# State added by one whole product, bonus vector spread behind the first token sums, and a new order of loads and steps

One core of one Trainium2 chip. The metric is the device time of one execution in microseconds (us); lower is better. A run counts as slow when it is more than 1.5% above the fastest run of the same kernel; fast runs are compared with fast runs.

## The reference

The kernel computes a linear attention with a decaying state (four batches, 8 heads of 48, 768 tokens) and feeds its output into a token-mixing layer.

```python
# attention, per batch and head; w is the decay, u the bonus vector
for t in range(S):
    cur = einsum('bhd,bhe->bhde', u * k[t], v[t])
    y[t] = einsum('bhd,bhde->bhe', r[t], state + cur)
    state = w[t][..., None] * state + einsum('bhd,bhe->bhde', k[t], v[t])
# token mixing, x = y as (B, S, 384)
wq, wk = x @ w_q, x @ w_k
W_tok  = scale * einsum('bsd,btd->bst', wq, wk)
out    = maximum(einsum('bst,btd->bsd', W_tok, x), 0) @ w_out
```

## The kernel before

It works on 12 blocks of 256 tokens, three to a batch. For each block: `load` fetches w, k, r and v, in this order, 384 KB each, from the sync engine's queue; `log` takes the logarithm of w on ScalarE; `sums` adds the logarithms up over the tokens on TensorE (tiles `cw`); `expk` and `expr` take exponentials of the sums; `kdec` (GpSimd, tile `KdS`) and `rdec` (VectorE, tile `RdS`) decay keys and receptances; `trR` transposes them (`psT`); then come two masked products (`A`, `AmB`), the state (`Sn`, `SB`) and the output `Y`. The bonus takes a second path: `uk1` and `uk2` on GpSimd, `red` on VectorE, `vd` on GpSimd.

```python
ld = ctx.enter_context(tc.tile_pool(name="ld", bufs=3))

def load(n, nm, ap):
    b, m = divmod(n, NU)
    src = ap[b, :, ds(m * C2, C2)]
    t = ld.tile([C, H, D2], F32, name=nm + "G", tag=nm + "G")
    nc.sync.dma_start(out=t, in_=src.rearrange("h (p j) d -> p h (j d)", j=2))
    T[nm, n] = t

def log(n):
    T["lw", n] = LW[n % NB]
    nc.scalar.activation(pad(T["lw", n]), jhd(T["w", n]), ACT.Ln, bias=0.0, scale=LN_SCALE)

def stadd(n, q):                       # adds the old state to the new one, in PSUM
    ...
        SB = T["SB", b, 2 * m + q]
        for hh in range(2):            # two products of 64 columns, side by side
            mm(T["Sn", n][ds(hh * 64, 64), q, 0:DM].rearrange(
                "p (q h d) -> p q h d", h=2, d=D)[:, :, hh],
               ID128[:, ds(hh * 64, 64)],
               SB.rearrange("p (q h d) -> p q h d", h=2, d=D)[:, :, hh], start=False)

def ucast():                           # spreads the bonus vector over 128 partitions
    ups = mtile([C, DM], F32, "ups")
    mm(ups, one, u1)
    nc.vector.tensor_copy(ubc, ups)
```

The order of instructions on each engine comes from a plan: every step has a key, and the steps are issued in the order of their keys. A key is not a time on the chip. It only decides who stands ahead of whom on an engine or in a queue.

```python
start  = [0.42, 8.84, 16.14, ...]                # key of each block; steps add to it
lstart = [-100, -99, -98, -11.4, -9.09, 4.54, 0.63, 6.68, 49.1, 51.23, 17.9, 58.9]
for n in range(NT):
    for i, (nm, ap) in enumerate((("w", w), ("k", k), ("r", r), ("v", v))):
        at(lstart[n] + 0.01 * i, lambda n=n, nm=nm, ap=ap: load(n, nm, ap))
    ...
at(-99.985, uload); at(-99.0, ucast); at(-67.84, wload); at(19.23, wcast)
for _, _, fn in sorted(plan, key=lambda x: x[:2]):
    fn()
```

So the blocks are loaded in the order 0, 1, 2, 3, 4, 6, 5, 7, 10, 8, 9, 11.

## Time and profile before

| | before |
|---|---|
| median of the first three runs | 123.15 us (122.78 to 123.25) |
| span of the profiled run | 122.0 us |
| TensorE busy | 100.1 us, 82% |
| VectorE, GpSimd, ScalarE busy | 91.8, 84.7, 77.2 us |
| TensorE almost without a gap (0.9 us of 56) | from about 44 to 100 us |

To read it: shares over the whole span hide stages. TensorE is the bound in the middle. The front, up to some 42 us, is bound by waits, by GpSimd and by the loads. The prediction shows the lines.

### The profile page before, as it was taken

The page shows a single profiled execution, that of the slowest core. Times are in us where ns is not written, and L with a number is a line of the kernel's source. Part 1 is how long each engine was busy: PE and PEld are TensorE (multiplying, and loading weights), DVE is VectorE, ACT ScalarE, POOL GpSimd, SP SyncE. Part 2 cuts the span into 40 slices and gives each one's busy share as a digit, 9 for nine tenths or more (in the row PEclk, how much of TensorE's full clock was granted, in tenths as well). Part 3 has the DMA queues.
Part 4 walks back from the last instruction along what each step waited for, and adds up shares of the span by engine and source line. Part 5 has one row for each costly group of instructions (what it writes and reads, how often), then busy time and mean ns, then how long its engine had stood idle before and what let it go on. Part 6 is the DMA issues. An engine that isn't in the chain of part 4 may idle for free.

```text
span 122.0 us, 4284 instructions
## 1 busy us (share of the span) xinstructions
PE 100.1 (82%) x1822; PEld 64.6 (53%) x1822; DVE 91.8 (75%) x150; ACT 77.2 (63%) x146; POOL 84.7 (69%) x81
## 2 busy tenths in 40 slices
PE   0193938979898999999999899999999999966800
PEld 0133536557575766757657466576576666532400
DVE  6213596699798978999989998989989777253800
ACT  4236391689779868986685948976478966426000
POOL 8949899995999999599597995967839804000000
PEclk9999996799999999999999999999999999999985
DMA  3999999999999999899839999500552200573092
GB/s 77 322 325 325 323 320 341 292 232 318 236 256 273 288 300 263 230 266 247 245 75 329 348 269 252 149 0 0 134 129 52 82 5 0 129 181 85 24 283 83
DMA packets 54598, 24.66 MB, mean 202 GB/s; under 512 B 51121, under 2 KB 54578, under 8 KB 54578
## 3 DMA queue, kind: packets, MB, share of 16 engines
q1 hardware_dynamic: 52274, 21.24, 64.6%
q10 hardware_dynamic: 2304, 3.15, 9.1%
q8 instruction: 14, 0.23, 0.7%
q14 instruction: 6, 0.05, 0.1%
HBM read 19.66 MB, written 4.72 MB: 200 GB/s over the span
## 4 chain that ended last, share of the span: by engine, by line
PE 68%; ACT 12%; DVE 6%; DMA 3%; POOL 3%; issue 2%; ACTq 1%; SPq 1%; DVEq 0%
PE cw L66 12%; PE Y L66 11%; PE psT L66 10%; PE fps L66 10%; PE Sn L66 5%; PE A L66 5%; PE xt_ps L66 5%; PE qk L66 5%; PE Tps L66 4%; ACT X L130 3%; DMA u<-in_u_dram 3%; DVE AmB L244 3%; ACT XT L130 2%; PE mps L66 2%; POOL uk L250 1%
## 5 line engine op out<-in xcount | busy, mean ns | idle before, releaser
L244 DVE TENSOR_TENSOR AmB<-A,MASK 128x1024 bf16<-128x1024 f32 x24 | 28.8, 1219 | 1.3 <-PE A L66 1.2
L271 POOL TENSOR_TENSOR Vd<-V,diag 128x768 bf16<-128x768 bf16 x12 | 17.7, 1478 | 13.7 <-ACT X L130 3.4
L250 POOL TENSOR_TENSOR uk<-kG,ubc 128x768 f32<-128x768 f32 x12 | 21.8, 1816 | 1.7 <-DVE ubc L486 1.7
L178 ACT ACTIVATE em<-cw,bias 128x384 bf16<-128x384 f32 x24 | 13.0, 580 | 15.6 <-PE cw L66 15.6
L257 POOL TENSOR_TENSOR uk<-uk,rG 128x768 f32<-128x768 f32 x12 | 21.8, 1816 | 0.1
L207 POOL TENSOR_TENSOR KdS<-kG,em 128x768 bf16<-128x768 f32 x12 | 19.7, 1640 | 1.2 <-ACT em L178 1.2
L227 DVE COPY RKT<-psT 128x2048 bf16<-128x2048 bf16 x12 | 14.6, 1217 | 4.0 <-PE psT L66 4.0
L66 PEld LDWEIGHTS <-KdS 64*128 64x128 bf16 (+1 forms) x256 | 10.8, 99 | 9.1 <-POOL KdS L207 3.6
L200 DVE TENSOR_TENSOR RdS<-rG,cw 128x384 bf16<-128x384 f32 x24 | 12.2, 551 | 4.5 <-ACT cw L185 4.5
L66 PE MATMUL fps<-wout_sb,mixT 128*128 128x384 bf16 x72 | 14.6, 328 | 0.1
L302 DVE TENSOR_TENSOR SB<-Sn,pt 128x384 bf16<-128x384 f32 x20 | 11.0, 551 | 4.0 <-PE Sn L66 2.6
L66 PEld LDWEIGHTS <-RKT 48*64 48x64 bf16 (+1 forms) x464 | 10.3, 107 | 7.1 <-issue 4.5
L185 ACT ACTIVATE cw<-cw,bias 128x384 f32<-128x384 f32 x24 | 12.3, 553 | 0.2
L264 DVE TENSOR_REDUCE diag<-uk 128x16 f32<-128x768 f32 x12 | 11.3, 945 | 0.4 <-POOL uk L257 0.4
L155 ACT ACTIVATE logw<-wG 128x768 bf16<-128x768 f32 x12 | 10.2, 851 | 2.1 <-DMA wG<-in_w_dram 2.1
L66 PE MATMUL cw<-logw,BI 128*128 128x384 bf16 x36 | 11.5, 377 | 0.0
L66 PE MATMUL psT<-ID,KdS 128*128 128x128 bf16 x96 | 7.8, 227 | 4.0 <-DVE AmB L244 2.0
L66 PE MATMUL cw<-logw,BS 128*128 128x384 bf16 x36 | 11.0, 363 | 0.0
L66 PE MATMUL A<-RKT 48*64 48x128 bf16 x384 | 10.1, 226 | 0.8 <-ACT X L130 0.8
L130 ACT CAST X<-Y 128x768 bf16<-128x768 f32 x11 | 8.8, 800 | 2.9 <-PE Y L66 2.7
L211 ACT CAST V<-vG 128x768 bf16<-128x768 f32 x12 | 10.0, 841 | 0.0
L130 ACT COPY osb<-fps 128x384 f32<-128x384 f32 x13 | 6.1, 484 | 5.3 <-PE fps L66 2.1
(74 smaller groups left out, 165.1 us busy)
## 6 DMA issues: line engine op xcount, KB each, us to landing
wG<-in_w_dram SPq DMA_DIRECT2D x12, 384.0 KB, 5.5
kG<-in_k_dram SPq DMA_DIRECT2D x12, 384.0 KB, 5.1
rG<-in_r_dram SPq DMA_DIRECT2D x12, 384.0 KB, 4.8
vG<-in_v_dram SPq DMA_DIRECT2D x12, 384.0 KB, 4.9
out_dram<-osb ACTq DMA_DIRECT2D x16, 192.0 KB, 3.0
out_dram<-osb SPq DMA_DIRECT2D x8, 192.0 KB, 3.8
wout_f<-in_moe_w_out_dram SPq DMA_DIRECT2D x1, 576.0 KB, 4.7
wq_f<-in_moe_w_q_dram SPq DMA_DIRECT2D x1, 96.0 KB, 4.1
```

The lines of the kernel that those rows point to most:

```text
L66: nc.tensor.matmul(o, l, rr, start=start, stop=stop, skip_group_check=True, is_transpose=trans)
L130: (nc.scalar.copy if e else nc.vector.tensor_copy)(o, i)
L178: nc.scalar.activation(em[:, j], T["cw", n, 1 + j][:, 0:DM], ACT.Exp, bias=bias[2 + j], scale=-1.0)
L185: nc.scalar.activation(cw, cw, ACT.Exp, bias=bias[j], scale=1.0)
L200: nc.vector.tensor_tensor(pad(Rd)[:, j], jhd(T["r", n])[:, j], T["cw", n, j][:, 0:DM].rearrange("p (h d) -> p h d", d=D), ALU.mult)
L207: nc.gpsimd.tensor_tensor(pad(T["Kd", n]), jhd(T["k", n]), hd(T["em", n]), ALU.mult)
L227: nc.vector.tensor_copy(RKT, T["psT", n])
L244: nc.vector.tensor_tensor(T["AmB", n][:, js].rearrange("p q h t -> p h q t"), T["A", n, js], _rep(_rep(MASK[:, js], 1, NP), 1, 2), ALU.mult)
L250: nc.gpsimd.tensor_tensor(uk, T["k", n].rearrange("p h (j d) -> p h j d", j=2), _rep(ubc.rearrange("p (h d) -> p h d", d=D), 2, 2), ALU.mult)
L257: nc.gpsimd.tensor_tensor(uk, uk, T["r", n].rearrange("p h (j d) -> p h j d", j=2), ALU.mult)
L264: nc.vector.tensor_reduce(diag.rearrange("p j h -> p h j"), T["uk", n], axis=AX.X, op=ALU.add)
L271: nc.gpsimd.tensor_tensor(Vd, T["V2", n], _rep(T["diag", n], 3, D), ALU.mult)
```

## The change

The intent has three parts. The addition of the old state becomes one full product instead of two half ones. The product that spreads the bonus vector moves behind the first token sums, and the first decayed keys (`kdec`) go ahead of the first bonus product (`uk1`), so that the first transposes could start earlier. Finally the whole plan is reordered, with the loads and the division of copies between ScalarE and VectorE.

```diff
-            for hh in range(2):
-                mm(T["Sn", n][ds(hh * 64, 64), q, 0:DM].rearrange(
-                    "p (q h d) -> p q h d", h=2, d=D)[:, :, hh],
-                   ID128[:, ds(hh * 64, 64)],
-                   SB.rearrange("p (q h d) -> p q h d", h=2, d=D)[:, :, hh], start=False)
+            mm(T["Sn", n][:, q, 0:DM], ID128, SB, start=False)
...
-    EX = (1, 1, 1, 1, 1, 1, 1, 1, 1, 1, 1, 0)      # 1: ScalarE copies X of this block
-    ET = (1, 1, 1, 1, 0, 0, 0, 0, 0, 1, 1, 0)      # the same for XT
+    EX = (0, 1, 1, 1, 1, 1, 1, 1, 1, 1, 1, 0)
+    ET = (0, 1, 1, 0, 0, 0, 0, 0, 1, 0, 1, 0)
...      (other such lists, every key of the steps, two checks of order, the layout of XT: left out)
     first = [                                      # keys of block 0
...
-        (0.59, uk1, ()),
-        (1.7, expr, ()),
-        (3.15, kdec, ()),
+        (-0.86, expr, ()),
+        (3.93, kdec, ()),
+        (5.41, rdec, ()),
+        (6.11, uk1, ()),
...
-    lstart = [-100, -99, -98, -11.4, -9.09, 4.54, 0.63, 6.68, 49.1, 51.23, 17.9, 58.9]
+    lstart = [-100, -99, -98, -37.57, -37.75, -19.78, -26.05, -25.0, 20.07, 36.92, -5.83, 30.2]
...
-    at(-99.0, ucast)
-    at(-67.84, wload)
-    at(19.23, wcast)
+    at(-5.72, ucast)
+    at(-74.79, wload)
+    at(15.4, wcast)
```

The new `lstart` loads the blocks in the order 0, 1, 2, 4, 3, 6, 7, 5, 10, 8, 11, 9.

## The prediction

> **What bounds the kernel now.** I read the page first: engine totals, then the slices, then the chain that ended last in order of time, then a table of windows, then the timeline of single engines. A block below is 256 tokens of one batch; there are 12, numbered 0 to 11, each passing through loads, exponentials, transposes, two masked products, the state and the output.
>
> ```profile
> PE 100.1 (82%) x1822; PEld 64.6 (53%) x1822; DVE 91.8 (75%) x150; ACT 77.2 (63%) x146; POOL 84.7 (69%) x81
> ```
>
> No engine is full over the span, so the averages hide stages. The windows (stretch, length, then busy us with counts of PE, PEld, DVE, ACT, POOL, then clock, DMA share, GB/s) separate them:
>
> ```profile
> 6.00:12.00 6.00, 4.13 (x24) 1.69 (x23) 1.58 (x3) 3.02 (x6) 4.30 (x4) 1.00 1.17 325
> 12.00:18.00 6.00, 4.15 (x58) 2.78 (x57) 4.22 (x5) 3.79 (x8) 5.39 (x4) 1.00 1.17 322
> 18.00:24.00 6.00, 5.30 (x87) 3.71 (x88) 4.03 (x6) 2.72 (x6) 6.00 (x5) 0.72 1.11 323
> ...
> 44.00:52.00 8.00, 8.00 (x161) 5.16 (x159) 6.97 (x11) 7.44 (x16) 6.52 (x5) 1.00 0.97 256
> ...
> 60.00:68.00 8.00, 8.00 (x184) 5.23 (x182) 7.57 (x11) 5.88 (x12) 7.20 (x5) 1.00 0.82 233
> ```
>
> From 44 us TensorE has no gap (8.00 of 8), with VectorE close behind (7.57 of 8 at 60 to 68). Before 24 us TensorE waits, GpSimd fills up (6.00 of 6) and the transfers run at 322 to 325 GB/s. So there are three stages: a front of some 42 us limited by waits, GpSimd and loads; a middle of some 64 us limited by TensorE; a tail. The front in the chain:
>
> ```profile
> 1.85 3.55 DMA u<-in_u_dram
> 5.40 0.14 issue
> 5.53 1.63 PE ups L66 x2
> 7.16 0.02 issue
> 7.18 0.57 DVE ubc L486
> 7.75 0.07 issue
> 7.83 1.81 POOL uk L250
> 9.64 1.60 POOL KdS L207
> 11.24 0.04 issue
> 11.29 1.89 PE psT L66 x16
> ...
> 26.67 0.26 ACT wq_sb L495
> 26.94 0.24 ACT wk_sb L496
> 27.18 1.05 ACT wout_sb L497
> ```
>
> The path starts with the bonus vector: its load, the product that spreads it, its copy, the keys times the bonus, and only then the decayed keys that the first transposes need. The casts of the weights are also on it, 1.55 us.
>
> **What the Trainium skill says.** (1) "TensorEngine Tiling (Array Packing)", Key Properties: changing the tiling mode drains TensorE. The trace agrees. Around one state addition of before (timeline of PE):
>
> ```profile
> 65.83 0.22 PE L66 MATMUL psT<-ID,RdS 128*128 128x128 bf16 x1
> 65.98 0.27 PE L66 MATMUL Sn<-SB,ID 128*64 128x192 bf16 x2
> 66.18 0.34 PE L66 MATMUL cw<-logw,BI 128*128 128x384 bf16 x1
> 66.36 0.33 PE L66 MATMUL cw<-logw,BS 128*128 128x384 bf16 x1
> ```
>
> The last transpose starts 0.15 us before the pair, where transposes of one mode follow each other after 0.056 us (eight of them last 0.61, one 0.22; 0.39/7). (2) "TensorE: Matmul & The Clock Gate", Part 3: outputs in different column groups run at the same time. Agrees: two products of 0.27 us together occupy 0.27 us, and the next starts 0.20 us after the first. (3) Same page, Back-to-back issue gap: N/2.4 + 2.5 ns when warm, 162 ns for N = 384. Agrees: cw products start 0.16 to 0.17 us apart. (4) "DMA: Bandwidth & Descriptors", anatomy of one DMA: about 2 us of each transfer are fixed. The rows here can't split it, but no load of keys landed under 4.0 us after issue (4.0/5.1/6.4, least, median, most).
>
> **The change part by part.**
>
> *State addition.* 16 additions (32 products in the row Sn<-SB,ID) become 16 products of 128 x 384. Streaming gets longer: 384 columns instead of two times 192 side by side, 0.16 against 0.08 us. Switches of mode get fewer. Between transposes and token sums: before 0.15 in, 0.20 out = 0.35; after 0.056 + 0.163 = 0.22, saving 0.136. After the state product (64-row mode) and before a full-array product: before 0.13 + 0.20 = 0.34, after 0.13 + 0.16 = 0.30, saving 0.04. Between two products of 64-row mode a switch is added: 0.13 + 0.16 + 0.095 = 0.39, losing 0.055 (0.095 is 0.15 less 0.055). In the new order of instructions I count 6 of the first kind, 4 of the second, 3 of the third, and three mixed ones worth -0.04, -0.04 and +0.06. Sum: -0.82 - 0.16 + 0.165 - 0.02 = -0.84 us; counting only blocks 4 to 11, where TensorE is the bound, about -0.45. The other reordering leaves the number of switches as it was (159 with the old addition, 141 with the new).
>
> *Front.* The first logarithm ends at 4.98, so the sums can start about 5.05 instead of 7.08, 2.0 us earlier. In before the second em (the exponential for the keys) ended 2.3 us after the sums' start (7.08 to 9.38); so em is done at 7.4, and the first decayed keys at 7.4 + 1.64 = 9.04 instead of 11.23. That is the intended gain, 2.2 us. But the bonus product now follows the sums (2.35 us, to 7.4) and takes its 1.63, then the copy 0.57: ubc is there at 9.6, where GpSimd, free at 9.04, waits 0.6. Its sequence then, with 1.81 for each product with the bonus or r, 1.64 for KdS, 1.48 for Vd: uk done 11.5, 13.3, 15.1, 16.9, keys of block 1 at 18.5, Vd 20.0, two uk of block 2 23.6, keys of block 2 25.2, Vd 26.7, two uk of block 3 30.3, Vd 31.8, keys of block 3 33.4, and keys of block 4 40.1. In before the keys were ready at 17.0, 25.0, 33.1 and 39.7. GpSimd as a whole is thus not ahead: the keys now come after both bonus products, and eat the lead. The transposes of blocks 3 and 4 began at 34.98 and 41.71, some 1.6 us after my new times, so at most 1.6 us can come out of the front.
>
> *Loads.* There are three buffers per input. The new order is 0, 1, 2, 4, 3, 6, 7, 5, 10, 8, 11, 9, so block 3 has one transfer group of 4 x 1.2 us ahead of it while the queue is full, and block 5 can be loaded only when block 4's keys are released. With 4.0 us to land: keys of 5 at 44.1, two products and the decay 5.25 us later 49.35; the transposes of block 5 began at 49.37. So by block 5 the lead from the front is about nil. If the keys of block 3 land at 28.4 (the fifth group's key issue 23.46 plus 4.9), GpSimd loses 1.7 more, and block 5 is late by as much. Block 9 has the same handicap (after 8), but GpSimd catches up about 1 us per block by then.
>
> *Moves between engines.* Three evacuations go from ScalarE to VectorE net (one X at 0.96 us instead of 0.80, two XT at 0.55 instead of 0.80), the relu, osb and qk counts stay. VectorE +2.1 us over the span, of which 1.5 falls on block 0, about 24 to 28 us, where it was full; between 60 and 84 us some 1.2 us are taken off it. The weights' casts move into ScalarE's wait before 21.8 us (-1.55 on the old path, though they now wait for the weights, which land about 20.2). Seven fewer stores are issued by ScalarE (about 0.6 each); only those at 105.6 to 106.9 stood on the chain, and X of the last block at 107.46 hid them anyway. The layout of XT moves the same elements in the same products: nothing.
>
> *Tail.* From the last Y (106.5) to 122 the order is nearly unchanged; one of six osb copies goes to ScalarE. I take -0.1.
>
> Sum by the walk: front 0 (-1.6 to +1.7), addition -0.45, tail -0.1: about 122.6. The walk charges every stall and gives nothing for the warm clock, and a new order this broad was most likely kept because it ran at least as well; I move 0.7 us for that, a judgement and not a reading: **121.9 us**.
>
> **Rivals.** (a) *The front gain carries through*: 2.2 + 1.55 us come off the chain and GpSimd's waits vanish. For: TensorE is solid behind it, so each microsecond survives. Against: GpSimd's sequence and DMA at 325 GB/s. It would give 119.5 to 120.5. (b) *Loads become the wait*: block 3 and block 5 late by 1 to 2 us, not regained because TensorE is the bound. For: GpSimd's arithmetic above. Against: 18 to 26 us has some idle transfer time. It would give 123.3 to 124.2. (c) *VectorE becomes the bound* around block 1 through the moved X and XT: for, it is full from 24 to 28 us; against, two state evacuations (0.55 each) now run earlier, in its idle time. +0.5 to 1.0, so 122.5 to 123.
>
> **Range and chances.** The walk's middle is 122.6, rival (a) pulls down 2 to 3, (b) up 1. Eight in ten: 120.0 to 123.5. Faster by over 2% needs under 120.7, so rival (a) nearly whole: 0.19. Slower by over 2% needs over 125.6, more than all stalls together: 0.03. Within 2%: 0.78.
>
> **What would show it.** Right if: the first sums start near 5.1, KdS of block 0 ends near 9.1; GpSimd waits about 0.6 for ubc; Sn<-SB,ID is 16 products of 128x384; PE is full from 44 to 100; transposes of block 5 start near 49 with POOL KdS as releaser of a wait of PE or its weight load. Wrong if those transposes start before 47.5 (the front gain held, so 120 us or less), if psT waits elsewhere for loads of block 9, or if TensorE's middle shrinks by over 1 us, which would mean that drains cost more than I counted.

## The result, and the profile after

The changed kernel is slower: 128.17 us, median of 4 runs (126.57 to 128.84), against 122.97 us for the kernel before on the same chip (122.71 to 123.25, 4 runs). The ratio is 1.034, 95% interval 1.0246 to 1.0435. Here and below a ratio is the mean time of one kernel's fast runs over that of the other's fast runs of the same rounds, so it is not quite the ratio of the medians quoted. Two of the four runs (128.84 and 128.58) count as slow; the fast ones took 126.57 and 127.75. The profiled run is the one of 128.84 us, span 126.7 us. What is read from it below was therefore looked for again in fast traces, and it is there (experiments `e2` and `e4`).

The engine totals hardly show where five microseconds went:

```profile
PE 101.7 (80%) x1806; PEld 65.2 (52%) x1806; DVE 94.2 (74%) x153; ACT 75.5 (60%) x143; POOL 85.0 (67%) x81
```

TensorE has 1.6 us more busy time with 16 instructions fewer, VectorE 2.4 us more. The windows after, with the columns the prediction explains, find the place:

```profile
6.00:12.00 6.00, 5.04 (x30) 2.20 (x29) 1.58 (x3) 3.97 (x8) 4.02 (x4) 1.00 1.17 325
44.00:52.00 8.00, 5.80 (x101) 3.22 (x102) 3.46 (x5) 5.63 (x10) 5.51 (x4) 0.79 0.72 193
60.00:68.00 8.00, 8.00 (x147) 5.31 (x146) 8.00 (x13) 4.96 (x10) 7.28 (x5) 1.00 0.73 199
```

The front is busier than before (5.04 instead of 4.13 us of TensorE's time). At 60 to 68 us TensorE is full, as before. But from 44 to 52 us it worked 5.80 us instead of 8.00, with 101 records instead of 161, and the granted clock was 0.79. The waits of the changed kernel (engine, line, what was waited for; total us, times, longest) name the wait:

```profile
ACT logw L157 <- DMA wG<-in_w_dram: 11.7, 6, 4.1
POOL uk L254 <- DMA kG<-in_k_dram: 9.1, 3, 4.5
...
PE cw L68 <- ACT logw L157: 8.9, 3, 5.1
```

ScalarE waited 11.7 us for loads of w; in the kernel before the same group has 2.1 us of idle time. Not all of this is loss: 3.1 us stand ahead of blocks 0 to 2 (a fast run with the old loads, `e6`, has the same 3.1), the rest is 2.96 ahead of block 3, 4.06 ahead of block 5 and 1.62 ahead of block 9. Behind ScalarE, TensorE's token sums waited for the logarithm; of these 8.9 us, 5.1 are the start of block 0, 0.96 block 1 and 2.88 block 5. Up to block 4 the changed kernel is all but level: its transposes of block 4 start at 41.98 us, before at 41.71. The chain that ended last (start, duration, what) puts it in one place, block 5:

```profile
39.36 5.82 DMA wG<-in_w_dram
45.18 0.02 issue
45.20 0.85 ACT logw L157
46.05 0.04 issue
46.09 2.04 PE cw L68 x15
48.13 1.90 PE Y L68 x40
```

One load of w, issued at 39.36 and landed at 45.18, holds up the logarithm, that the sums, and those TensorE. In the kernel before, the same logarithm ran on time; its timeline of ScalarE has it without a wait:

```profile
40.77 0.85 ACT L155 ACTIVATE logw<-wG 128x768 bf16<-128x768 f32 x1
```

The same stretch of the chain of before has no load and no wait in it:

```profile
43.08 1.20 PE cw L66 x15
44.28 1.22 PE Y L66 x40
```

The first sums of block 5 start at 46.09 instead of 42.91 us, which is 3.2 us later. The products behind them are slow on top. From the start of the sums to the start of `Y` it is 1.98 us instead of 1.30, and from there to the next product 1.87 instead of 1.21. (The chain of before enters the sums only at 43.08, because their first 0.17 us lie beside the last transposes; its 1.20 us are therefore not the whole of them.) Together that is 3.2 + 0.7 + 0.7, about 4.5 us, and the transposes of block 5 start 4.7 us later, first after, then before:

```profile
54.02 0.62 PE L68 MATMUL psT<-ID,KdS 128*128 128x128 bf16 x8
```

```profile
49.30 0.62 PE L66 MATMUL psT<-ID,KdS 128*128 128x128 bf16 x8
```

Why the slow products? The timeline of TensorE shows the idle time ahead of the sums, and windows of one microsecond show the clock after it (the third number from the end):

```profile
46.09 0.32 PE L68 MATMUL cw<-logw,BI 128*128 128x384 bf16 x1 [2.88 <-ACT logw L157]
```

```profile
43.00:44.00 1.00, 0.21 (x4) 0.09 (x2) 1.00 (x3) 0.00 (x0) 0.00 (x0) 1.00 1.12 298
...
46.00:47.00 1.00, 0.91 (x4) 0.48 (x4) 0.00 (x0) 1.00 (x4) 0.59 (x1) 0.70 0.54 148
47.00:48.00 1.00, 1.00 (x12) 0.39 (x10) 0.00 (x0) 1.00 (x3) 1.00 (x1) 0.50 0.03 8
49.00:50.00 1.00, 1.00 (x12) 0.30 (x14) 0.83 (x2) 0.25 (x1) 1.00 (x1) 0.59 1.17 325
50.00:51.00 1.00, 0.90 (x24) 0.43 (x23) 0.59 (x1) 0.94 (x3) 1.00 (x2) 1.00 1.14 318
```

The clock reads 1.00, then 0.70, 0.50 and 0.59, and 1.00 again. After 2.88 us without a product and the first sums, TensorE worked at half clock from 46.4 to 49.8 us (worked out from the windows: a mean of 0.70 is 0.60 us at half clock, a mean of 0.59 is 0.82 us). The Trainium skill, "TensorE: Matmul & The Clock Gate", Part 1, says that the array falls to half clock after about one idle window of 3.4 us and warms up after as long a busy one. The trace agrees in the half clock and in its length, 3.4 us (the fast traces of `e2` and `e4` also have 3.4); the idle time ahead of it was shorter than the page says. How much the late start costs and how much the clock is read from the trace; no run separates the two.

Why did w of block 5 come so late? The timeline of the sync engine's queue has its issue, behind block 7's four loads; the second view is the issue of the same w before:

```profile
33.19 1.17 SPq L152 DMA_DIRECT2D wG<-in_w_dram  x1
...
38.23 1.08 SPq L152 DMA_DIRECT2D vG<-in_v_dram  x1
39.36 1.46 SPq L152 DMA_DIRECT2D wG<-in_w_dram  x1
```

```profile
33.60 1.37 SPq L150 DMA_DIRECT2D wG<-in_w_dram  x1
```

The seventh group of loads starts at 33.19 and the eighth at 39.36; before, they start at 33.60 and 39.34. The queue runs at the same pace in both kernels. Only, before, block 5 is the seventh group, and now it is the eighth, since 7 was put ahead of it. That moves its w by 39.36 - 33.60 = 5.8 us, and there were not 5.8 us to spare.

### The profile page after: what moved, and what is told of

Its sections match the earlier page's. It is cut to its first block, busy times and chain, and to the rows that moved or that the text cites. A ratio compares the mean times of both kernels' runs of the same rounds, so it can differ in the third digit from the quotient of the medians.

```text
span 126.7 us, 4242 instructions
## 1 busy us (share of the span) xinstructions
PE 101.7 (80%) x1806; PEld 65.2 (52%) x1806; DVE 94.2 (74%) x153; ACT 75.5 (60%) x143; POOL 85.0 (67%) x81
## 3 DMA queue, kind: packets, MB, share of 16 engines
q10 hardware_dynamic: 1296, 1.77, 5.2%
## 4 chain that ended last, share of the span: by engine, by line
PE 54%; DMA 12%; SPq 9%; ACT 9%; DVE 6%; issue 3%; POOL 1%; DVEq 0%; ACTq 0%; POOLq 0%
PE Y L68 10%; PE cw L68 9%; DMA wG<-in_w_dram 8%; SPq L152 8%; PE fps L68 8%; PE psT L68 8%; PE Sn L68 4%; PE qk L68 4%; DMA rG<-in_r_dram 4%; PE A L68 3%; PE xt_ps L68 3%; ACT X L132 3%; PE Tps L68 2%; PE mps L68 2%; DVE AmB L247 2%
## 5 line engine op out<-in xcount | busy, mean ns | idle before, releaser
L68 PE MATMUL cw<-logw,BI 128*128 128x384 bf16 x36 | 11.7, 384 | 8.9 <-ACT logw L157 8.9
L157 ACT ACTIVATE logw<-wG 128x768 bf16<-128x768 f32 x12 | 10.2, 846 | 12.2 <-DMA wG<-in_w_dram 11.7
L68 PEld LDWEIGHTS <-KdS 64*128 64x128 bf16 (+1 forms) x256 | 11.3, 101 | 6.7 <-issue 2.5
L68 PE MATMUL cw<-logw,BS 128*128 128x384 bf16 x36 | 11.5, 377 | 0.0
L268 DVE TENSOR_REDUCE diag<-uk 128x16 f32<-128x768 f32 x12 | 11.3, 945 | 0.0
L132 ACT CAST X<-Y 128x768 bf16<-128x768 f32 x10 | 8.0, 798 | 3.3 <-PE Y L68 3.3
L418 ACT ACTIVATE mixT<-mps 128x384 bf16<-128x384 f32 x18 | 8.1, 495 | 2.5 <-PE mps L68 2.4
```

What stands on the lines that cost most here:

```text
L68: nc.tensor.matmul(o, l, rr, start=start, stop=stop, skip_group_check=True, is_transpose=trans)
L132: (nc.scalar.copy if e else nc.vector.tensor_copy)(o, i)
L268: nc.vector.tensor_reduce(diag.rearrange("p j h -> p h j"), T["uk", n], axis=AX.X, op=ALU.add)
```

## The experiments

Each "before" median is on the same chip. Calls ran on different chips: `e1` to `e4`, `e5` to `e8`, `e9` to `e12` and `e13` to `e16` belong together.

The theory after reading the trace: the order of loads alone makes the loss. The rivals: the moved bonus product and key order, the copies moved to VectorE, or too few load buffers.

**e1: the changed kernel with the loads in the old order.**

```diff
-    lstart = [-100, -99, -98, -37.57, -37.75, -19.78, -26.05, -25.0, 20.07, 36.92, -5.83, 30.2]
+    lstart = [-100, -99, -98, -11.4, -9.09, 4.54, 0.63, 6.68, 49.1, 51.23, 17.9, 58.9]
```

> The changed kernel with only the list of load times put back to that of before (blocks loaded 0,1,2,3,4,6,5,7,10,8,9,11). Theory L (the new load order is the whole loss: w of block 5 lands at 45.2 us and w of block 9 at 76.3 us, and each wait lets TensorE go idle and cold): 121.0 to 123.0 us, no DMA wait of a logarithm after the first, TensorE without a gap from 44 us. Theory S (the new order on the engines, keys after both bonus products, X and XT of block 0 on VectorE, loses the time, and the loads are only where it shows): still 126 or more. A share for both: 123.5 to 125.5.

Measured: fast runs 123.78 and 123.68 us, before 123.54; ratio 1.0015 (0.9958 to 1.0071). Two more runs were slow (126.84 and 134.24). The loss is gone, so it sits in `lstart`. What remains of the change is worth nothing within 0.6%. Two fast runs are few, but `e6` and `e7` below, which have the same old loads, bear it out with six fast runs each.

The run of 134.24 us is the profiled one. Its window from 60 to 68 us has a granted clock of 0.75 where other runs have 1.00, and this went on to the end.

```profile
60.00:68.00 8.00, 8.00 (x127) 5.03 (x125) 7.22 (x11) 3.92 (x8) 5.61 (x4) 0.75 0.67 179
```

**e2: the kernel before with the loads in the new order** (the same line, the other way round).

> The kernel before with only the list of load times of the change. Theory L: 126 to 129 us, with the logarithm of block 5 waiting 3 to 5 us for its w. Theory S: within 1% of before, 122 to 124.2, since the keys come early in this order and give their buffer back early. A share for both: 124.3 to 126.

Measured: 128.41, 129.28 and 128.70 us fast, 130.96 slow; median 128.99, before 123.54; ratio 1.0425 (1.0373 to 1.0477). One line of keys makes the kernel before as slow as the changed one, and a little slower. Its trace is of a fast run and its chain shows the same wait:

```profile
39.66 5.55 DMA wG<-in_w_dram
...
45.24 0.85 ACT logw L155
```

Here TensorE had been idle for 3.47 us, and all of its sums ran at half clock: they took 2.31 us, and the first ones started 0.27 and 0.32 us apart, where before it was 0.16. With `e1` and `e2` the cause is shown from both sides.

**e3: the kernel before with the whole addition alone.**

```diff
-            for hh in range(2):
-                mm(T["Sn", n][ds(hh * 64, 64), ...  # two products
+            mm(T["Sn", n][:, q, 0:DM], ID128, SB, start=False)
```

> The kernel before with only the state addition as one product of 128x384. The tiling drains saved less the longer streaming: my count gives 0.5 to 0.9 us less, so 122.0 to 122.6 where before has 123.0. If the drains cost nothing and only streaming counts: 0.08 us times 16 more, 124.2. If nothing of it lies on the path: 123.0.

Measured: median of 6 is 122.32 us (121.80 to 122.92), before 123.54; ratio 0.9907 (0.9869 to 0.9945), about 1.15 us. The addition is a real gain of its own. TensorE's timeline shows the working of one addition:

```profile
65.14 0.61 PE L66 MATMUL psT<-ID,RdS 128*128 128x128 bf16 x8
65.58 0.33 PE L66 MATMUL Sn<-SB,ID 128*128 128x384 bf16 x1
65.75 0.33 PE L66 MATMUL cw<-logw,BI 128*128 128x384 bf16 x1
```

The product stands 0.17 us ahead of the token sums; the pair of before stood 0.20 ahead, for half the columns. Read off single starts: from the last transpose to the addition 56 ns instead of 149, and from the addition to the sums 162 instead of 203. The way in is what became cheap.

**e4: the changed kernel with four load buffers.**

```diff
-    ld = ctx.enter_context(tc.tile_pool(name="ld", bufs=3))
+    ld = ctx.enter_context(tc.tile_pool(name="ld", bufs=4))
```

> The changed kernel, its new load order kept, with four buffers per input instead of three. Theory L in its exact form (not the order as such, but that block 5 and block 9 must wait for the buffer of block 4 and block 8): the waits vanish, 121.0 to 123.0 us. If the order itself hurts through the queue (block 4 ahead of block 3 while the transfers are full): about 1.8 us of wait for the keys of block 3 stays and it gives 123 to 124.5. Theory S: 126 or more.

Measured: 127.95, 129.17 and 127.75 us fast, 130.04 slow; median 128.56, before 123.54; ratio 1.0398 (1.0324 to 1.0471). More room does not help. The queue's timeline in this fast run shows why:

```profile
38.40 1.04 SPq L152 DMA_DIRECT2D vG<-in_v_dram  x1
39.49 1.14 SPq L152 DMA_DIRECT2D wG<-in_w_dram  x1
```

w of block 5 is issued at 39.49 as soon as v of block 7 is out, and landed 5.72 us later. It waited for its turn, not for a buffer. The keys of block 5 do need a buffer: with three, they were issued at 41.91 us, right after block 4's keys were released at 41.88. With four they went out at 40.72 and came into use no sooner (46.43 us, with three 46.41). A later wait did vanish: the logarithm of block 9, last in the order, no longer waits (1.62 us with three buffers), and `Y` of block 11 starts at 109.1 instead of 109.9 us, this one against a slow trace; the total shows no gain from it. So the queue bounds block 5 and the buffers block 9.

**e5: the changed kernel, block 5 put ahead of block 7 in the loads.**

```diff
-    lstart = [-100, -99, -98, -37.57, -37.75, -19.78, -26.05, -25.0, 20.07, 36.92, -5.83, 30.2]
+    lstart = [-100, -99, -98, -37.57, -37.75, -25.5, -26.05, -25.0, 20.07, 36.92, -5.83, 30.2]
```

> The changed kernel with one block moved in its load order: 5 ahead of 7, so 0,1,2,4,3,6,5,7,10,8,11,9. Four buffers did not help block 5, whose w still landed at 45.2 us while transfers ran without a pause, so for block 5 it is the place in a full queue and not the buffer. Theory Q (place in the queue): w of block 5 is issued near 33 instead of 39.4, lands before 40 us, TensorE does not stop before the token sums of block 5, and 3 to 4.5 us come back: 123.5 to 125.5 in fast runs; what stays of the wait is block 9 (about 1 us). Theory B (buffer release): nothing changes, 126.5 to 128.8.

Measured: two fast runs, 123.89 and 124.59 us, two slow (127.85 and 126.90); before 123.56. Two fast runs out of four are too few for a ratio with an interval; their mean over the median of before is 1.0055. One number out of the whole plan takes back most of the loss. In the trace (fast) w of block 5 is issued at 33.34, its logarithm runs without a wait, and the sums start at 43.2 us:

```profile
41.18 0.85 ACT L157 ACTIVATE logw<-wG 128x768 bf16<-128x768 f32 x1
```

**e6: e1, with the weights' casts where they were.**

```diff
-    at(15.4, wcast)
+    at(19.23, wcast)
```

> The changed kernel with the old load order, and the casts of the weights put back behind the transposes' copy of block 0 as in before. The first run with the old load order came out level with before although the one-product addition alone brought 0.9%; about 1% is lost elsewhere. If it is the early casts (ScalarE stands 1.9 + 1.8 us for the weights' load and the exponentials of block 2 wait behind it): 0.5 to 1.2 us below the run with old loads alone, so 122.3 to 123.0. If X and XT of block 0 on VectorE are the loss: no change, 123.5, or up to 1 us slower since the casts are then again ahead of the logarithm of block 3.

Measured: 6 fast runs, median 123.78 us, before 123.56; ratio 1.0007 (0.9980 to 1.0033). The early casts, which the prediction credited with 1.55 us "on the old path", bring nothing that can be seen beside `e1`, whose interval is 0.6% to either side.

**e7: e1, with X and XT of block 0 copied by ScalarE again.**

```diff
-    EX = (0, 1, 1, 1, 1, 1, 1, 1, 1, 1, 1, 0)
-    ET = (0, 1, 1, 0, 0, 0, 0, 0, 1, 0, 1, 0)
+    EX = (1, 1, 1, 1, 1, 1, 1, 1, 1, 1, 1, 0)
+    ET = (1, 1, 1, 0, 0, 0, 0, 0, 1, 0, 1, 0)
```

> The changed kernel with the old load order, and X and XT of block 0 evacuated by ScalarE again. In the changed kernel VectorE is full from 24 to 30 us and X and XT of block 0 (0.87 and 0.46 us) stand on the chain between the masks of block 1. If they are the loss: 1.0 to 1.4 us less, 122.1 to 122.6. If the early casts are: no change, 123.5.

Measured: 6 fast runs, median 122.95 us, before 123.56; ratio 0.9950 (0.9918 to 0.9982). That is 0.6% below `e1` (1.0015) and `e6` (1.0007; it differs in the place of the casts too, which brings nothing visible in `e6`), so about 0.75 us; the intervals of `e6` and `e7` just touch. The chain of the changed kernel shows what the two copies cost on VectorE:

```profile
24.47 0.87 DVE X L132
25.34 1.13 DVE AmB L247
26.47 0.46 DVE XT L132
26.94 1.14 DVE AmB L247
```

All four stand on the path one behind the other. With the copies away, in the trace of `e7`, the masks start at 25.25 and 26.66 us, where `e6` has 25.48 and 27.08; they now wait 0.60 and 0.18 us for `A`, so not all of the copies' 1.3 us comes back.

**e8: e3 with the new start: bonus product behind the first sums, first keys ahead of the bonus.**

```diff
-        (0.59, uk1, ()),
         (1.7, expr, ()),
         (3.15, kdec, ()),
+        (3.2, uk1, ()),
...
-    at(-99.0, ucast)
+    at(-5.5, ucast)
```

> The kernel before with the one-product addition and only the new start: bonus product behind the first token sums, first keys decayed ahead of the first bonus product; nothing else moved. If the start is what bounds (chain read as it stands): 2 us less than the addition alone (122.3), so 120.2 to 121. If GpSimd's sequence bounds the front (walk of the prediction: it starts 0.4 us earlier but then waits 0.6 for the bonus): within 0.5 us of 122.3.

Measured: 6 fast runs, median 122.58 us, before 123.56; ratio 0.9919 (0.9889 to 0.9948), the same as `e3`. The first transposes start at 9.0 instead of 11.3 us, and yet nothing is gained: `Y` of block 0 still starts at 23.0 (before 22.9). VectorE's timeline shows where the 2.3 us end:

```profile
14.90 0.95 DVE L264 TENSOR_REDUCE diag<-uk 128x16 f32<-128x768 f32 x1 [2.15 <-POOL uk L257]
15.77 1.01 DVE L200 TENSOR_TENSOR RdS<-rG,cw 128x384 bf16<-128x384 f32 x2
16.70 2.35 DVE L244 TENSOR_TENSOR AmB<-A,MASK 128x1024 bf16<-128x1024 f32 x2
```

The bonus sum of block 0 (`diag`) stands ahead of the masks in VectorE's order. It waits 2.15 us for GpSimd's bonus products, which now come later, and all that stands behind it waits too.

**e9: e8, with the bonus sum of block 0 behind its masks, and `vd` earlier.**

```diff
-        (9.1, red, ()),
         (12.22, mask, (1, )),
+        (12.25, red, ()),
...
+        (14.3, vd, ()),
-        (16.87, vd, ()),
```

> The kernel before with the one-product addition, the new start, and the sum over the bonus product of block 0 moved on VectorE from ahead of the masks of block 0 to behind them (its product with the values moved along on GpSimd). In the run with the new start alone the first transposes begin at 9.0 instead of 11.3 but the masks still at 16.7, because that sum stands ahead of them on VectorE and waits for GpSimd until 14.9. Theory F (VectorE's fixed order hands the lead back): masks of block 0 start near 15.0, transposes of block 1 near 16.5 instead of 18.0, Y of block 0 near 22 instead of 23, and 0.8 to 1.8 us come off: 120.8 to 121.8. Rival (loads or the cold clock of TensorE bound the front): token sums of block 2 stay at 20.7 and the time at 122.4.

Measured: 5 fast runs, 121.85, 121.47, 121.11, 120.69 and 121.60 us, one slow (125.12, the profiled one); before 123.62; ratio 0.9812 (0.9776 to 0.9848). Now the earlier start counts. The order can be seen in the fast trace of `e10`, which has the same one:

```profile
14.10 1.03 DVE L200 TENSOR_TENSOR RdS<-rG,cw 128x384 bf16<-128x384 f32 x2 [1.22 <-ACT cw L185]
15.05 2.35 DVE L244 TENSOR_TENSOR AmB<-A,MASK 128x1024 bf16<-128x1024 f32 x2
17.31 0.94 DVE L264 TENSOR_REDUCE diag<-uk 128x16 f32<-128x768 f32 x1
```

The masks begin at 15.05 instead of 16.70, and `Y` of block 0 starts at 21.5 us in this trace and at 21.0 in that of `e9`, where `e8` had 23.0.

The slow trace of `e9` shows the wait of the changed kernel again, here with the old order of loads. w of block 5 was issued at 36.30 us (before: 33.60), the logarithm waited for it, and TensorE stood idle and then ran at half clock from 44.1 to 47.5 us:

```profile
43.13 0.84 ACT L155 ACTIVATE logw<-wG 128x768 bf16<-128x768 f32 x1 [4.22 <-DMA wG<-in_w_dram]
```

```profile
44.02 0.47 PE L66 MATMUL cw<-logw,BI 128*128 128x384 bf16 x1 [3.04 <-ACT logw L155]
```

**e10: e9, with the cast of the output weights in three parts, placed later.**

```diff
-        nc.scalar.copy(wout_sb, wout_f)
+
+    def wocast(i):
+        nc.scalar.copy(wout_sb[:, i], wout_f[:, i])
...
+    for i, t in enumerate((26.5, 30.3, 33.65)):
+        at(t, lambda i=i: wocast(i))
```

> As the run before it in this list, with the cast of the output weights (1.15 us on ScalarE at 27 us, on the chain ahead of the logarithm of block 3) cut in three and put into ScalarE's gaps behind the logarithms of blocks 3 and 4. If that cast bounds: 0.5 to 1.1 us less again. If the masks on VectorE or the keys on GpSimd bound there: no change.

Measured: median of 6 is 121.87 us (120.93 to 122.29), before 123.62; ratio 0.9844 (0.9803 to 0.9885). No gain over `e9`.

**e11: e9 without the new start**, that is e3 with the moves of `red` and `vd` alone (the same diff as e9, on e3).

> The kernel before with the one-product addition and the moved sum on VectorE, but with the old start (bonus product first). With theory F the lead does not exist here: the masks wait for A at 15.3 to 16.2 and start near 16.0 behind RdS of block 1, as now, at most 0.6 us better: 121.8 to 122.5. If the moved sum alone is worth as much as with the new start (under 121.5), the start has no share.

Measured: 122.04 to 123.77 us, median 122.22, before 123.62; ratio 0.9904 (0.9860 to 0.9948), the same as `e3`. So the start alone gives nothing (`e8`), the order on VectorE alone gives nothing, and the two together give 0.9% more than the addition by itself (`e9` against `e11`, whose intervals just miss each other). The later kernels with both, `e10`, `e13` and `e14`, lie 0.3 to 0.7% below `e11`, so the size of this gain is not settled.

**e12: the changed kernel, with 5 ahead of 7 and 9 ahead of 11 in the loads.**

```diff
-    lstart = [-100, -99, -98, -37.57, -37.75, -19.78, -26.05, -25.0, 20.07, 36.92, -5.83, 30.2]
+    lstart = [-100, -99, -98, -37.57, -37.75, -25.5, -26.05, -25.0, 20.07, 29.0, -5.83, 30.2]
```

> The changed kernel, its own load order but with 5 ahead of 7 and 9 ahead of 11 (0,1,2,4,3,6,5,7,10,8,9,11). If these two places are the whole of the loads' loss: level with the changed kernel on the old load order, 123.3 to 123.9, and no more runs above 126. If block 4 ahead of block 3 also costs (GpSimd waits 1.8 us for the keys of block 3): 0.3 to 1 us above that.

Measured: only two fast runs, 124.62 and 124.31 us, and four slow ones (127.06 to 128.66); median 127.21, before 123.62. The fast mean over the median of before is 1.0068. What still differs in the loads from `e1` is 4 ahead of 3. Its trace (fast) has ScalarE waiting 3.65 us for w of block 3 and GpSimd 2.50 us for its keys. The swap of 9 and 11 shows no gain over `e5` in these few runs.

**e15 and e16: e12 again, one run each, to catch a slow run in a trace.**

> The changed kernel with 5 ahead of 7 and 9 ahead of 11, again, for its trace. If it comes out near 127: the trace shows a wait for block 3's or block 5's data of 3 us or more and TensorE cold behind it (loads), or else PE busy with a lower granted clock throughout (chip). If near 124.5: nothing new.

> As the second look: near 127 with a load's wait of over 3 us if loads make the slower runs, or a low clock throughout if the chip does; near 124.5 tells nothing.

Measured: 124.39 and 124.98 us, correct, the state of single runs unknown; the median of before in this call was 123.41. Neither is as slow as the slow runs of `e12`, so no trace of one exists. Why the kernels with block 4 loaded ahead of block 3 fell into slow runs so often (`e5` 2 of 4, `e12` 4 of 6) stays open. The two kept traces of slow runs with the old order of loads differ: that of `e9` has the late w of block 5, that of `e1` a lower clock and no such wait. So neither the loads nor the clock is shown to be the cause of all of them.

**e13 and e14: the two best kernels with the blocks loaded in their order 0 to 11** (`e13` is `e9`, `e14` is `e10` with this line).

```diff
-    lstart = [-100, -99, -98, -11.4, -9.09, 4.54, 0.63, 6.68, 49.1, 51.23, 17.9, 58.9]
+    lstart = [-100, -99, -98, -11.4, -9.09, 0.63, 4.54, 6.68, 17.9, 49.1, 51.23, 58.9]
```

> The kernel of the start with VectorE's order put right, now with all blocks loaded in their order of use. If the place in the queue is what its slower run (125.1) met: no wait of a logarithm for w after block 2 above 1 us, all runs within 1%, 120.5 to 121.3. If the 125.1 was a slow state of the chip: median as before, 121.5, and again a run near 125.

> The kernel with the split cast of the output weights, with blocks loaded in their order of use. If the loads hid the gain of the split cast (its logarithm of block 5 waited for w until 41.5): 0.5 to 1 us below the run before it in this list, 119.7 to 120.7. If the cast was never on the path: level with it.

Measured against 123.41 us: `e13` median of 6 is 121.91, ratio 0.9878 (0.9843 to 0.9913); `e14` median of 5 is 121.30, ratio 0.9837 (0.9811 to 0.9862). Neither had a slow run, and in the trace of `e13` the logarithm of block 5 does not wait (in `e10`, with the old order, it waits 1.75 us). `e14` is level with `e10`, `e13` lies 0.7% above `e9`, with intervals that just touch: plain order shows no gain, and a small cost is not ruled out. `e9` and `e14` have overlapping intervals, and both beat both kernels: about 1.6 to 1.9% below before. No version is clearly more than 2% faster than before.

## Why the prediction was wrong

The prediction was 121.9 us, with 120.0 to 123.5 as its range, and gave a loss of over 2% a chance of 0.03. The changed kernel took 126.57 and 127.75 us in its fast runs.

**The step that failed is "Loads".** It reads: "block 5 can be loaded only when block 4's keys are released", and concludes "by block 5 the lead from the front is about nil", with up to 1.7 us of lateness in the bad case. Three things in it did not hold.

1. It followed only the keys of block 5, to their transposes at 49.4 us. (Those came late too, in use at 46.41 us instead of 44.1: 1.8 us because block 4's keys were released late, 0.5 in landing.) But w is the first tensor of a block that is needed: its logarithm ran at 40.77 us, over 8 us ahead of those transposes. The load of w landed at 45.18, and this is the 3.2 us of late sums. The prediction never compared the landing of w with the time at which its logarithm was due.
2. It took the release of a buffer for the limit. For the keys of block 5 that held, but for w it did not: in `e4` a fourth buffer left w of block 5 at 39.49 to 45.21; the limit was the place in the queue. Putting block 7 ahead of block 5 cost block 5 a whole group. The Trainium skill, "DMA: Bandwidth & Descriptors", Queues, rings and completion order, says that the descriptors on an engine's ring are consumed in order; the trace shows order one step earlier, at the issue, 33.60 against 39.36 us for the same w.
3. It had no term for a cold clock behind a wait. An idle time of 2.88 us (3.47 in `e2`, 2.44 in `e4`) was followed by half clock, and the sums and `Y` took 1.3 us longer from start to start (0.68 and 0.66).

None of it is seen to be regained: in `e2` the transposes of block 5 start 4.4 us late (53.71 against 49.30) and the fast runs are 5.2 us longer. TensorE has few gaps behind it, as the prediction said of the middle ("each microsecond survives"; its "no gap" from 44 us was 0.9 us of gaps up to 100). A further, smaller loss comes at the end, at block 9: by the one trace of `e4` up to 0.8 us, which its total does not show.

**The judgement had the wrong sign.** The prediction took off 0.7 us because "a new order this broad was most likely kept because it ran at least as well". The order of the loads ran worse by 4.25% (`e2`). With the loads set back the changed kernel is at 1.0007 (`e6`), and this has the gain of the addition in it, 0.93% by `e3`; so the rest of the new order lost about 1.2 us. A guess about why someone kept an order is no reading.

**Rival (b), "Loads become the wait", was right in kind.** It was sized at 123.3 to 124.2 us, with "block 3 and block 5 late by 1 to 2 us". Block 5 was late by 4.7; block 3 was not (transposes at 35.25 us, before 34.98), although ScalarE and GpSimd waited for its loads.

What was right, step by step (the timeline of GpSimd in the changed kernel):

```profile
7.43 1.63 POOL L210 TENSOR_TENSOR KdS<-kG,em 128x768 bf16<-128x768 f32 x1 [1.32 <-ACT em L180]
9.63 1.81 POOL L254 TENSOR_TENSOR uk<-kG,ubc 128x768 f32<-128x768 f32 x1 [0.57 <-DVE ubc L492]
...
28.45 1.81 POOL L254 TENSOR_TENSOR uk<-kG,ubc 128x768 f32<-128x768 f32 x1 [1.77 <-DMA kG<-in_k_dram]
...
46.41 1.81 POOL L254 TENSOR_TENSOR uk<-kG,ubc 128x768 f32<-128x768 f32 x1 [4.53 <-DMA kG<-in_k_dram]
```

- *The front.* The first decayed keys end at 9.06 us (predicted 9.04), and GpSimd waits 0.57 for the bonus (0.6). The keys of blocks 1 to 4 end at 18.57, 25.25, 35.19 and 41.88 us. Predicted were 18.5, 25.2, 33.4 and 40.1, and for the case of late keys of block 3 another 1.7 us; that case came true, with a wait of 1.77. The first sums start at 5.1 us as said.
- *The lead is handed back.* `Y` of block 0 starts at 22.8 us, before at 22.9. The prediction put this down to GpSimd's order, and in the changed kernel the transposes of block 1, at 18.63 us, do wait for GpSimd's keys (they end at 18.57). But most of the lead is spent before that, on TensorE, which the prediction did not look at. The new plan puts the sums of block 1 ahead of the first transposes, and these start at 12.02 us although their keys are ready at 9.06; before, they started at 11.29 (after, then before; the fast trace of `e6`, with the same order, has 12.07):

```profile
9.91 0.48 PE L68 MATMUL cw<-logw,BI 128*128 128x384 bf16 x1 [0.96 <-ACT logw L157]
...
12.02 1.06 PE L68 MATMUL psT<-ID,KdS 128*128 128x128 bf16 x8
```

```profile
11.29 1.03 PE L66 MATMUL psT<-ID,KdS 128*128 128x128 bf16 x8 [1.87 <-POOL KdS L207]
```

  `e8` and `e9` have another order on TensorE (first transposes at 9.0 us). They show a third place, VectorE: there the bonus sum ahead of the masks stops the lead (`e8`), and with it moved the lead gets through (`e9`). In the changed kernel that sum does not wait, and the masks start at 15.97 us, before at 16.90; this rest of the lead is lost at GpSimd's keys.
- *The check at block 5.* The transposes of block 5 were to start near 49 us, released by GpSimd's decayed keys. They started at 54.0. The keys of block 5 were in use from 46.41 us (estimated landing: 44.1) and decayed at 51.7, so they were late too, by 2.3 us, but TensorE was later still.
- *The addition.* Gaps into and out of one product came out as predicted (56 and 162 ns, 0.22 together; after a state product 135 and 173; between two 64-row products 135 and 269). `e3` gives 0.93%, about 1.15 us (by its interval 0.7 to 1.6). The total of -0.84 us lies within that; the -0.45 that went into the sum, "counting only blocks 4 to 11", was too small.
- *Rival (c), VectorE around block 1.* Predicted +0.5 to 1.0 us; `e7` finds about 0.75. Right in size. With the gain of the addition, -1.15, that makes -0.4 us, where `e6` finds +0.1; the other 0.5 us of the new order was not traced to a step.
- *The casts.* Moving them shows no gain (`e6` against `e1`), against the 1.55 us that rival (a) gave them; the sum of the walk had left them out.

## What to carry to other kernels

When an order of loads in a full queue is changed, take every tensor of every block, add its landing time, and compare it with its first consumer; the earliest-needed tensor decides (here w, 8 us ahead of the transposes that looked critical), and more buffers do not help a load that waits for its turn. A lead on one engine counts only if no instruction of fixed order on the next engine waits in front of it, so follow it engine by engine until it reaches the bound, and move what stands in the way. When one full product can replace a pair of half-width ones between full-width neighbours, the saved switches can outweigh the longer streaming (here 0.9% for one line).

## What the Trainium skill lacked or had wrong

- "TensorEngine Tiling (Array Packing)", Key Properties, says that a change of mode drains TensorE, but gives no size. Here the last transpose stood 149 ns ahead of a 128x64 pair against 56 ns ahead of a full product, and the pair 203 ns ahead of the next full product (some 80 of it for its 192 columns, by the 162 ns that 384 columns took).
- "TensorE: Matmul & The Clock Gate", Part 1, gives an idle window of about 3.4 us for the fall to half clock. Its table for kernels ("Why this matters for your kernels") asks for no gaps over about 3 us. Here shorter gaps did it too: half clock set in with the gap of 2.88 us (after its first sums, which were still 0.16 to 0.17 us apart), with 3.47 us in `e2` and with only 2.44 us in `e4` (in both the first sums were already about 0.3 us apart). So the length of the gap alone did not decide.
- The same part knows full and half clock, 13/16 for a die with three busy cores, and a clock seen stuck at a quarter. One run of this one-core kernel (`e1`, 134.24 us) had a granted clock of 0.75 from about 23 us to the end, but for 3.4 us at 0.50 in between, and 0.75 is none of these.
- "DMA: Bandwidth & Descriptors" gives the order in a ring, but not what decided here: with the queue kept full, 384 KB loads were issued 1.1 to 1.2 us apart at best and moved at up to 325 GB/s, and landed 5.5 to 5.8 us after issue. A block of four loads put ahead therefore cost the next block 5.8 us.
